# GEGLU feed-forward on one core: w_gate's first quarter in two transfers, x's second half released one transfer earlier in ACT's program

## The chip, the cores and the metric

The kernel runs on one core of a Trainium2 chip. The metric is the device time in microseconds (us) of one execution; the number quoted for a kernel is the median of several runs. Engines are named as the profile names them: PE (TensorE, matmuls; PEld is its weight loads), DVE (VectorE), ACT (ScalarE), POOL (GpSimd), SP (SyncE). A trailing q (ACTq, SPq) means the engine's instruction queue, which also issues DMA transfers.

## The reference

```python
B, S, D, F = 32, 32, 1024, 3584          # all bfloat16
def reference(x, w_gate, w_up, w_down):
    return (gelu_tanh(x @ w_gate) * (x @ w_up)) @ w_down
```

x is flattened to 1024 rows of D = 1024. w_gate and w_up are 1024 x 3584, w_down is 3584 x 1024.

## The kernel before, in words

The three products are done by a fast (Strassen-like, seven-product) scheme on two-by-two blocks. For the first two matrices the blocks are: x's first 512 rows and its other 512 rows, by the first and second half of D. In the code xt0 holds the transposed first 512 rows: B11 is its first half of D (KH = 4 steps of 128, called dt), B21 its second half. xt1 holds the other 512 rows (B12, B22). The 28 blocks of 128 columns of F (FT = 28) are the outer loop. A tile of w_gate, WG[c], holds 256 columns, so two blocks, with 8 dt; its first four dt meet B11 and its last four meet B21. A third stage multiplies by w_down.

The schedule is written out by hand: each engine executes its instructions in the order of the program text, and the queues of SP and ACT issue their transfers in that order as well. Semaphores are put in for data that one engine waits for from another.

The start, which is where the change lies, goes as follows.

- **SP** issues the transposing load of x's first half, B11 (L131). Its next transfer is the transposing load of x's second half, B21 (L149); after that come w_gate 2's second half, half of w_up 0, w_gate 3's second half, w_gate 4, the transposing load of xt1 (L154), w_gate 5 in two halves and the rest of w_up 0.
- **PE** runs NWARM = 10 matmuls on constants (L137), numbered n = 0 to 9, into four PSUM tiles in turn.
- **ACT** copies a little of warm product 1 into `table` (L139), which also holds its queue until that product is done. Then it issues six loads of w_gate (line L86 in the helper `load_gate`): w_gate 0's dt 0 and 1 (128 KB), its dt 2 and 3 (128 KB), the first four dt of w_gate 1, 2 and 3 (256 KB each), and w_gate 0's last four dt (256 KB). Then a second copy (L139 again, n = 8) waits for warm product 8, a copy of eight columns from `table` into B21 (L147) follows, and a Gelu on constants (L148) makes ACT load its Gelu table.
- The copy into B21 is called the *touch* below. The touch writes into the tile that x's second half is loaded into, so SP has to wait for it before it issues L149. It is what sets the moment of that load.
- **PE** then does `first_products(0, 1, cuts=(0, 2, KH))` (L279): blocks 0 and 1, both on w_gate 0, side by side: dt 0 and 1 of block 0, dt 0 and 1 of block 1, then dt 2 and 3 of each. All these matmuls have the line L195, in the helper `pair_product`. ACT copies each finished product to E1 (L212) and issues w_gate 1's second half (L280). Blocks 2 to 7 follow one by one with four matmuls each, so the first products of blocks 0 to 7 are 32 matmuls. Then `second_products(0)` to `second_products(7)` add B21 times the second half of each w_gate tile; the results go through Gelu on ACT (L219).
- **DVE** meanwhile makes sums of w_gate and w_up for blocks 0 and 1 (L175 to L184) and, once xt1 has landed, the sums T1 to T4 of the blocks of x (L166), which the remaining products read.

Of the kernel before, what the change touches and what calls it, by code (L numbers as in the profile page):

```python
# [7 lines left out]
ACT = mybir.ActivationFunctionType  # L8
# [4 lines left out]
def kernel(  # L13
# [18 lines left out]
    nc = tc.nc  # L32
# [11 lines left out]
    KH = DT // 2  # L44
# [31 lines left out]
    B11, B21 = xt0[:, :KH, :], xt0[:, KH:, :]  # L76
# [6 lines left out]
    def load_gate(c, queue, lo=0, hi=DT):  # L83
        if c not in WG:
            WG[c] = gw.tile([P, DT, 2 * P], bf16, name="gw", tag="gw")
        queue.dma_start(  # L86
            out=WG[c][:, lo:hi, :], in_=wg_r[:, lo:hi, 2 * c * P : (2 * c + 2) * P]
        )
# [12 lines left out]
    def a11(i):  # L101
        return block(WG, 2, i, 0)
# [21 lines left out]
    def psum_p(name):  # L124
        return psum.tile([P, NB], fp32, name=name, tag="p")

    def psum_q(name):
        return psum.tile([P, NB], fp32, name=name, tag="q")

    with tc.manual_schedule():  # L130
        nc.sync.dma_start_transpose(out=B11, in_=xf[0:NB, 0 : KH * P])  # L131
        ones = nc.const_aps.tensor(1.0, [P, NB], bf16)
        warm = [psum_p("warm") for _ in range(4)]
        table = opool.tile([P, 8], bf16, name="table", tag="o")

        for n in range(NWARM):
            nc.tensor.matmul(warm[n % 4], lhsT=ones[:, 0:P], rhs=ones, start=True, stop=True)  # L137
            if n in (1, 8):
                nc.scalar.activation(table, warm[n % 4][:, 0:8], ACT.Copy)  # L139
            if n == 1:  # L140
                load_gate(0, nc.scalar, 0, 2)
                load_gate(0, nc.scalar, 2, KH)
                for c in (1, 2, 3):
                    load_gate(c, nc.scalar, 0, KH)
                load_gate(0, nc.scalar, KH, DT)
            if n == 8:
                nc.scalar.activation(B21[:, 0, 0:8], table, ACT.Copy)  # L147
                nc.scalar.activation(table, ones[:, 0:8], ACT.Gelu_apprx_tanh)  # L148
        nc.sync.dma_start_transpose(out=B21, in_=xf[0:NB, KH * P : D])  # L149
        load_gate(2, nc.sync, KH, DT)  # L150
# [12 lines left out]
        def t_sum(name, a, b, step=2):  # L163
            for k in range(0, KH, step):
                ks = slice(k, k + step)
                nc.vector.tensor_tensor(T[name][:, ks, :], a[:, ks, :], b[:, ks, :], ALU.subtract)  # L166
# [24 lines left out]
        def pair_product(ps, lhs, rhs, first, cuts):  # L191
            for lo, hi in zip(cuts, cuts[1:]):
                for p, l in zip(ps, lhs):
                    for k in range(lo, hi):
                        nc.tensor.matmul(  # L195
                            p,
                            lhsT=l[:, k, :],
                            rhs=rhs[:, k, :],
                            start=(first and k == 0),
                            stop=(k == KH - 1),  # L200
                            skip_group_check=True,
                        )

        def first_products(*blocks, cuts=(0, KH)):
            for i in blocks:
                A[i] = psum_p("a") if 4 <= i < 8 else psum_q("a")
            pair_product([A[i] for i in blocks], [a11(i) for i in blocks], B11, True, cuts)
            for i in blocks:
                if i % 2 == 0:
                    pool, tag = (xpool, "e1") if i == LEAD - 2 else (ring, "ring")  # L210
                    E1[i // 2] = pool.tile([P, 2, NB], fp32, name="e1", tag=tag)
                nc.scalar.activation(E1[i // 2][:, i % 2, :], A[i], ACT.Copy)  # L212
# [63 lines left out]
        t_sum("T2", B22, T["T1"])  # L276
        t_sum("T3", B22, B12)
        t_sum("T4", B21, T["T2"])
        first_products(0, 1, cuts=(0, 2, KH))  # L279
        load_gate(1, nc.scalar, KH, DT)  # L280
        for n in range(2, 8):
            first_products(n)
# [39 lines left out]
        for i in range(2, FT + 1):  # L322
# [24 lines left out]
            if here and i % 2 == 0:  # L347
                c = i // 2 + (6 if i < 8 else 4)
# [8 lines left out]
        for i in range(RING):  # L357
            lo, hi = 4 * i, min(4 * i + 4, KF)
            nc.sync.dma_start(out=V11[i][:, : hi - lo, :], in_=wd_r[:, lo:hi, 0:DB])
        for j in range(JF):  # L360
            lo = KF + 2 * j
# [31 lines left out]
        B21 = lambda j: V21[j]  # L393
# [149 lines left out]
```

## Time and profile before

| | |
|---|---|
| median of 3 runs | 275.68 us (275.56 to 275.73) |
| the profiled execution | 275.76 us, of which the span of its instructions is 273.9 us |
| granted TensorE clock (mean) | 1.000 |
| PE busy | 268.7 us |
| ACT busy | 139.7 us |
| DMA read and written | 22.02 MB, 2.10 MB |
| warm matmuls start | 0.77 us |
| first real matmul starts | 5.41 us |
| second products start | 12.99 us |

All later times are from the start of the span. A line of the timeline has start, duration, engine, source line, operation, what is written and read, and in brackets how long the engine stood idle before it and what ended that idleness. In the chain of waits a line has start, duration and what held the end of the program in that time. A transfer has a time of issue, which is when its instruction starts on its queue, and a time of landing, which is when its semaphore is raised; the trace records both, and the starts of the single packets between them. The end of a matmul is modelled: matmuls overlap, and in a steady stream of these shapes they start 0.216 us apart though each is drawn 0.38 us long. An idle time of PE in a view is counted from the modelled end and is therefore shorter than the time lost between starts.

### The profile page before, as it was taken

The page shows a single profiled execution, that of the slowest core. Times are in us where ns is not written, and L with a number is a line of the kernel's source. Part 1 is how long each engine was busy: PE and PEld are TensorE (multiplying, and loading weights), DVE is VectorE, ACT ScalarE, POOL GpSimd, SP SyncE. Part 2 cuts the span into 40 slices and gives each one's busy share as a digit, 9 for nine tenths or more (in the row PEclk, how much of TensorE's full clock was granted, in tenths as well). Part 3 has the DMA queues.
Part 4 walks back from the last instruction along what each step waited for, and adds up shares of the span by engine and source line. Part 5 has one row for each costly group of instructions (what it writes and reads, how often), then busy time and mean ns, then how long its engine had stood idle before and what let it go on. Part 6 is the DMA issues. An engine that isn't in the chain of part 4 may idle for free.

```text
span 273.9 us, 3338 instructions
## 1 busy us (share of the span) xinstructions
PE 268.7 (98%) x1172; PEld 189.4 (69%) x1186; DVE 189.2 (69%) x226; ACT 139.7 (51%) x240; POOL 87.2 (32%) x81
## 2 busy tenths in 40 slices
PE   8999999999999999999999999999999999999995
PEld 2445677778777787776877768764447888888883
DVE  0078885866658666586665866769994999999900
ACT  4778665566565665666655666531100072860311
POOL 0000075745557455584555845600000000000000
PEclk9999999999999999999999999999999999999999
DMA  7999402153300034216360202369602000000321
GB/s 185 277 288 247 154 1 77 52 180 110 121 2 0 0 103 130 77 35 196 96 213 0 77 5 74 107 190 334 214 0 77 2 0 1 0 2 0 116 77 38
DMA packets 41024, 26.42 MB, mean 96 GB/s; under 512 B 9264, under 2 KB 41008, under 8 KB 41008
## 3 DMA queue, kind: packets, MB, share of 16 engines
q1 hardware_dynamic: 37680, 24.51, 30.5%
q10 hardware_dynamic: 3328, 1.70, 2.3%
q8 instruction: 9, 0.15, 0.2%
q14 instruction: 7, 0.06, 0.1%
HBM read 22.02 MB, written 2.10 MB: 88 GB/s over the span
## 4 chain that ended last, share of the span: by engine, by line
PE 94%; DMA 4%; ACT 1%; issue 0%
PE x L195 19%; PE x L398 18%; PE y L115 18%; PE a L195 15%; PE y L398 9%; PE x L115 9%; PE z L398 4%; DMA xt<-in_x_dram 3%; DMA gw<-in_w_gate_dram 1%; PE y L195 1%; ACT L139 0%; ACT o_sb L510 0%
## 5 line engine op out<-in xcount | busy, mean ns | idle before, releaser
L195 PE MATMUL x<-T,s 128*128 128x512 f32 x224 | 63.4, 407 | 0.0
L195 PEld LDWEIGHTS x<-T,s 128*128 128x128 f32 x224 | 41.7, 188 | 10.9 <-ACT e L242 0.3
L195 PE MATMUL a<-xt,gw 128*128 128x512 bf16 x182 | 44.1, 380 | 1.1 <-DMA xt<-in_x_dram 0.3
L259 DVE TENSOR_TENSOR u<-y,e 128x512 bf16<-128x512 f32 x28 | 19.3, 691 | 31.8 <-ACT e L257 30.9
L184 POOL TENSOR_TENSOR s<-gw,s 128x512 fp32r<-128x512 bf16 x22 | 26.0, 1182 | 47.6 <-PE y L115 46.9
L180 DVE TENSOR_TENSOR s<-s,gw 128x512 fp32r<-128x512 f32 x24 | 34.9, 1456 | 0.0
L195 PEld LDWEIGHTS <-gw 128*128 128x128 bf16 x192 | 17.1, 98 | 24.8 <-issue 5.2
L266 ACT ACTIVATE gl<-h 128x512 bf16<-128x512 bf16 x28 | 17.7, 631 | 27.5 <-DVE h L264 27.5
L246 DVE TENSOR_TENSOR gT<-gl,x 128x512 bf16<-128x512 bf16 x28 | 19.2, 686 | 17.9 <-PE x L115 17.9
L115 PE MATMUL x<-T,c 128*128 128x512 f32 x112 | 30.3, 392 | 0.0
L115 PE MATMUL y<-B,s 128*128 128x512 f32 x112 | 30.2, 391 | 0.0
L175 POOL TENSOR_TENSOR s<-uw 128x512 fp32r<-128x512 bf16 x25 | 29.1, 1165 | 0.0
L115 PE MATMUL y<-T,s 128*128 128x512 f32 x104 | 27.8, 389 | 0.0
L398 PE MATMUL x<-tc,sc 128*128 128x512 f32 x112 | 25.7, 389 | 0.0
L257 ACT ACTIVATE e<-x 128x512 f32<-128x512 f32 x28 | 16.7, 600 | 16.0 <-PE x L195 16.0
L176 POOL TENSOR_TENSOR s<-gw,uw 128x512 fp32r<-128x512 bf16 x21 | 24.5, 1167 | 0.0
L115 PEld LDWEIGHTS y<-B,s 128*128 128x128 f32 x112 | 21.0, 188 | 4.8
L212 ACT ACTIVATE e<-a 128x512 f32<-128x512 f32 x28 | 16.6, 597 | 15.2 <-PE a L195 15.2
L115 PEld LDWEIGHTS x<-T,c 128*128 128x128 f32 x112 | 20.9, 188 | 4.8 <-ACT e L257 0.4
L398 PEld LDWEIGHTS x<-tc,sc 128*128 128x128 f32 x112 | 21.0, 188 | 4.4
L115 PEld LDWEIGHTS y<-T,s 128*128 128x128 f32 x104 | 19.5, 188 | 4.1
L219 ACT ACTIVATE gl<-a 128x512 bf16<-128x512 f32 x28 | 16.7, 597 | 7.1 <-PE a L195 7.0
(58 smaller groups left out, 342.0 us busy)
## 6 DMA issues: line engine op xcount, KB each, us to landing
uw<-in_w_up_dram SPq DMA_DIRECT2D x6, 1024.0 KB, 6.4
gw<-in_w_gate_dram SPq DMA_DIRECT2D x8, 512.0 KB, 4.0
v<-in_w_down_dram SPq DMA_DIRECT2D x5, 512.0 KB, 3.8
v<-in_w_down_dram SPq DMA_DIRECT2D x4, 640.0 KB, 8.1
v<-in_w_down_dram SPq DMA_DIRECT2D x8, 256.0 KB, 4.2
out_dram<-o_sb SPq DMA_DIRECT2D x15, 128.0 KB, 1.7
gw<-in_w_gate_dram ACTq DMA_DIRECT2D x5, 256.0 KB, 5.0
uw<-in_w_up_dram SPq DMA_DIRECT2D x2, 512.0 KB, 5.4
```

Of the source, the lines that this page charges most:

```text
L115: nc.tensor.matmul(ps, lhsT=lhs[:, k, :], rhs=rhs[:, k, :], start=(first and k == 0), stop=(k == KH - 1), skip_group_check=True,)
L175: engine.tensor_tensor(S1[i], a21(i), a22(i), ALU.add)
L176: engine.tensor_tensor(S3[i], a11(i), a21(i), ALU.subtract)
L180: nc.vector.tensor_tensor(S2[i], S1[i], a11(i), ALU.subtract)
L184: engine.tensor_tensor(S4[i], a12(i), S2[i], ALU.subtract)
L195: nc.tensor.matmul(p, lhsT=l[:, k, :], rhs=rhs[:, k, :], start=(first and k == 0), stop=(k == KH - 1), skip_group_check=True,)
L219: nc.scalar.activation(GL[i // 2][:, i % 2, :], A[i], ACT.Gelu_apprx_tanh)
L246: nc.vector.tensor_tensor(gT[:, i, 0:NB], GL[i // 2][:, i % 2, :], X[i], ALU.mult)
L257: nc.scalar.activation(e3, X[i], ACT.Copy)
L259: nc.vector.tensor_tensor(U1[i], Y[i], e3, ALU.add)
L266: nc.scalar.activation(G1[i], h1, ACT.Gelu_apprx_tanh)
L398: nc.tensor.matmul(ps, lhsT=lhs[:, i, t * P : (t + 1) * P], rhs=rhs[:, i, :], start=(first and j == 0 and i == 0), stop=(last and j == JF ...
```

## The change

Three edits, all in the first microseconds of the program.

1. w_gate 0's first four dt are loaded in three transfers, not two: dt 0 alone (64 KB), dt 1 alone (64 KB), dt 2 and 3 (128 KB).
2. `first_products(0, 1)` is cut at each of the first two dt: dt 0 of block 0, dt 0 of block 1, dt 1 of block 0, dt 1 of block 1, then dt 2 and 3 of each. Number and kind of matmuls are the same.
3. The second copy from a warm product (n = 8) is dropped, and the touch of B21 is moved in ACT's program from behind all the w_gate loads to behind w_gate 2's first half. Behind it come w_gate 3's first half, w_gate 0's second half and the Gelu on constants.

```diff
         for n in range(NWARM):
             nc.tensor.matmul(warm[n % 4], lhsT=ones[:, 0:P], rhs=ones, start=True, stop=True)
-            if n in (1, 8):
-                nc.scalar.activation(table, warm[n % 4][:, 0:8], ACT.Copy)
             if n == 1:
-                load_gate(0, nc.scalar, 0, 2)
-                load_gate(0, nc.scalar, 2, KH)
-                for c in (1, 2, 3):
-                    load_gate(c, nc.scalar, 0, KH)
+                nc.scalar.activation(table, warm[n][:, 0:8], ACT.Copy)
+                for lo, hi in ((0, 1), (1, 2), (2, KH)):
+                    load_gate(0, nc.scalar, lo, hi)
+                load_gate(1, nc.scalar, 0, KH)
+                load_gate(2, nc.scalar, 0, KH)
+                nc.scalar.activation(B21[:, 0, 0:8], table, ACT.Copy)
+                load_gate(3, nc.scalar, 0, KH)
                 load_gate(0, nc.scalar, KH, DT)
-            if n == 8:
-                nc.scalar.activation(B21[:, 0, 0:8], table, ACT.Copy)
                 nc.scalar.activation(table, ones[:, 0:8], ACT.Gelu_apprx_tanh)
...
-        first_products(0, 1, cuts=(0, 2, KH))
+        first_products(0, 1, cuts=(0, 1, 2, KH))
```

## The prediction

> **What bounds the kernel now.** I read the page's head first. TensorE (PE) is busy for 98% of the span, so a change pays only through the few moments at which PE stands still. PE's waits come next, in the second fence.
>
> ```profile
> span 273.9 us, 3338 instructions
> PE 268.7 (98%) x1172; PEld 189.4 (69%) x1186; DVE 189.2 (69%) x226; ACT 139.7 (51%) x240; POOL 87.2 (32%) x81
> ```
> ```profile
> PE a L195 <- DMA xt<-in_x_dram: 0.3, 1, 0.3
> PE a L195 <- DMA gw<-in_w_gate_dram: 0.2, 1, 0.2
> ```
>
> These two lines are all that PE waits for from 5 to 13.1 us (total, times, longest); from 13 us to the end the same view has only the tail of the x wait. So all that can be won lies ahead of 13 us. The chain of waits, 0 to 20 us, says by what:
>
> ```profile
> 1.83 3.54 DMA gw<-in_w_gate_dram
> 5.37 0.05 issue
> 5.41 0.26 PE a L195
> 5.67 7.18 DMA xt<-in_x_dram
> 12.86 0.14 issue
> 12.99 1.67 PE a L195 x7
> ```
>
> w_gate's first piece lands at 5.37 and the products begin; x's second half, issued at 5.67, lands at 12.86, and the second products begin at 12.99. The timeline shows who does what in between:
>
> ```profile
> 2.29 2.83 ACTq L86 DMA_DIRECT2D gw<-in_w_gate_dram  x5
> ...
> 5.23 0.18 ACT L139 ACTIVATE table<-warm 128x8 bf16<-128x8 f32 x1 [3.03 <-PE warm L137]
> 5.41 7.30 PE L195 MATMUL a<-xt,gw 128*128 128x512 bf16 x32 [0.21 <-DMA gw<-in_w_gate_dram]
> 5.44 0.21 ACT L147 ACTIVATE xt<-table 128x8 bf16<-128x8 bf16 x1
> 5.67 3.97 SPq L149 DMA_TRANSPOSE xt<-in_x_dram  x1
> ```
>
> The touch of B21 (L147) runs 5.44 to 5.65, and SP issues x's second half at 5.67. The 32 first products start 0.216 us apart; the last starts at 12.33, so PE could start the second products at 12.55. They start at 12.99: **0.44 us lost to x**. Within the first products PE loses 0.17 us before w_gate 0's dt 2 and 3 (landed 6.41) and 0.03 before w_gate 1 (landed 7.31).
>
> Last, the DMA queues by stretch (q10 is ACT's, q1 is SP's): first the answer for 4.4 to 8.5 us, then for 9.3 to 11.0.
>
> ```profile
> q10 hardware_dynamic: 2400, 1.19, 111.4%
> ```
> ```profile
> q1 hardware_dynamic: 1540, 0.39, 107.9%
> ```
>
> Between 4.4 and 8.5 not one packet of x moves, though x was issued at 5.67 and the first half of x had its first packet 1.41 us after its issue. Between 9.3 and 11.0 only x moves, though w_gate 1's second half was issued on ACT at 7.54. The transfers go one after the other, in the order of issue, across both queues. In the trace the w_gate pieces land at 5.37, 6.41, 7.31, 8.21, 9.12 and, for w_gate 0's second half, 9.88; then x.
>
> **The change, part by part.**
>
> *The split quarter.* The first piece has half the bytes. Its packets cannot start before 4.21, when x's first half leaves the engines. Before, 128 of w_gate's packets (64 KB) were through by 4.49 and 256 by 4.70, and the landing came 0.6 after the last; so the new first piece lands near 5.1 (x's first half: 4.97) and the second at 5.4. Two matmuls run in each step, then PE waits for dt 2 and 3 as before. This early start is worth nothing: from w_gate 1's landing at 7.31 there are 24 matmuls, 7.36 + 24 x 0.216 = 12.54, which is already the end of the first products. Only an earlier w_gate 1 would move it. The extra transfer delays what is queued behind it by an amount that I call delta. Upper bound: the 128 KB piece landed 1.04 after the piece before it, where 256 KB pieces come 0.90 apart; by bytes it should be 0.45, so a boundary between small pieces may cost 0.59. Lower bound: that pause belongs to the start of the stream and not to the boundary, and smaller pieces fill it; w_gate 1 would then land up to 0.45 sooner. The later boundaries show none of it, and 64 KB of w_gate's packets took 0.27 us: I take delta = 0.1, nearer to the rows of the long stream.
>
> *The issues on ACT.* One more issue goes ahead of w_gate 1. Five took 2.83 us, 0.57 each. Packets of a plain load follow their issue by 1.05 us in a quiet stretch (40.8); w_gate 1's would be issued near 3.5 and is not due on the engines until about 5.2. Covered by 0.6 us.
>
> *The touch.* It no longer waits for the ninth warm matmul (3.03 us of idle ACT), and follows five issues in place of six and that wait: 1.83 + 0.43 + 4 x 0.57 = 4.54, and 0.24 for the touch: x can be issued at 4.8 (4.5 if the 64 KB issues are as short as 0.37, the shortest in the trace, 5.0 if as long as 0.64). One thing limits this. The trace gives each transfer a semaphore for its landing; the first eight have eight different ones and the ninth has the first's again. With one transfer more, x's second half or w_gate 0's second half is the ninth, and would wait until x's first half lands, 4.97. So x is issued at 4.8 to 5.1. The copy that is dropped (0.18) ran on an idle ACT: nothing.
>
> *The order of the transfers.* w_gate 3's first half is issued from 4.56 on, beside the touch, so still ahead of x; w_gate 0's second half follows at about 5.13, now behind x. x moves ahead of one transfer worth 0.76 to 0.91 us, and lands at about 12.0 instead of 12.86. PE asks for it at 12.55 + delta: 0.5 us of cover. The whole 0.44 goes.
>
> *What is late next.* w_gate 0's second half is needed at 12.55 too. It follows x, whose packets end at 11.03 - 0.85 = 10.2; 0.82 for its packets and 0.73 to its landing (what w_gate 1's second half took at 11.01): 11.7, cover 0.8. w_gate 1's second half keeps its place (12.58; needed at 12.55 + 8 x 0.216 = 14.3). SP is freed sooner, since x's issue holds it until the queue ahead drains (9.65 before), but all it issues then queues on engines that are busy anyway. The Gelu table load (5.67) stays behind two issues, 4.56 + 2 x 0.57 = 5.7; its cover is that the first result comes at 7.08.
>
> *Does it reach the end?* After 13 us PE waits for nothing. The nearest deadline is VectorE's chain on x's other rows, landed 21.43: the fourth T1 quarter is done at 24.02 and PE reads it near 25.4; the first half of T2 at 25.16 for 26.74. PE can come 1.3 us earlier before anything there decides.
>
> Sum against the profiled execution (275.76 us, span 273.9, 1.9 around it): -0.44 + 0.1 = -0.34. Against the median of 275.68: **275.35**, -0.12%. A measurement of this kernel can tell about 0.2%, 0.55 us, from no change.
>
> **The rivals.**
>
> *The stream starts better (faster).* If the pause at the first boundary goes, w_gate 1 lands at 6.9 to 7.1 and the first products end at 12.1 to 12.35; x at 12.0 just keeps up. -0.44 - 0.2 to -0.45: 274.8 to 275.05. For it: DMA throughput falls from 370 to under 200 GB/s in the 0.4 us after the first piece, and a stretch so thin need not recur. Against: w_gate's bytes ahead of w_gate 1 stay the same.
>
> *x passes w_gate 3 as well (slower).* w_gate 3 is issued only some 0.2 us before x. If x is taken first, its packets (2.4 us, 8.6 to 11.03) go between w_gate 2 and 3. It decides once w_gate 3 lands after 10.8, when PE reaches its 25th product. x from 7.5 to 9.9, 0.82 for w_gate 3, 0.73 to the landing: 11.5. Second products start at 11.5 + 0.05 + 8 x 0.216 = 13.3: +0.3. With x as late as 7.9 and the landing lag that x itself had (1.0, after 0.75 between its last data and its semaphores) 12.3 and +1.1. Middle +0.6: 276.25. Against it: the order of issue held throughout the trace.
>
> *Each small piece pays its boundary (no change, or slower).* With delta at its upper bound of 0.59, w_gate 1 lands at 7.9, the first products end at 13.13 and x is there long before: 13.13 against 12.99, +0.15: 275.85. For it stands the 1.04 us of the one 128 KB piece, against it the full rate at all later boundaries.
> The Trainium skill leans this way: its page "DMA: Bandwidth & Descriptors", section "Bandwidth", calls transfers under 64 KB dominated by descriptors and has 64 KB take 0.95 us (loads issued from GpSimd there). By that, an estimate, two pieces would hold w_gate 1 up by some 0.9 us and make it 276.15; the 0.27 us above disagrees.
>
> *x stays last (no change).* w_gate 0's second half is issued at about 5.1, x between 4.8 and 5.1; a plain load has packets after 1.05 us and x after 1.41. If readiness and not issue sets the order, x gains nothing but the gap of 0.35 us in its own stream near 9.5: 275.4 to 275.8.
>
> **How the numbers follow.** Forecast 0.38, better stream 0.26, x ahead of w_gate 3 0.17, small pieces 0.09, x last 0.10. Faster by over 0.2% (below 275.13): nearly all of the better stream and a small part of the forecast with a negative delta, 0.30. Slower by over 0.2% (above 276.23): over half of x ahead of w_gate 3 (0.10), and 0.08 for a delta at or above its upper bound together with a w_gate 3 or x that is late as well, 0.18. Within: 0.52. Range 274.8 to 276.25: the better stream's end, and the middle of the slower case, which leaves out about 0.1 above and less below; the forecast's own range is 275.15 to 275.7.
>
> **What would show it.** Right: x's second half issued at 4.8 to 5.1 with the wait for warm gone from ACT, x landing near 12.0, PE's x wait gone, second products starting at 12.6. First matmul near 5.15 and a longer wait for w_gate inside the first products show that the split gives nothing. Wrong: w_gate 1 landing more than 0.2 us away from 7.31, a PE wait near 10.8 for w_gate 3, x packets still behind w_gate 0's second half, or a new PE wait after 13 us.

## The result and the profile after

The changed kernel takes 280.00 us (median of six, 278.50 to 281.13) against 275.71 us: 1.0145 times as long, 95% interval 1.0105 to 1.0184. The forecast of 275.35 and its range were wrong. The profiled execution, 278.50 us, is the fastest of the six; the rest of this section reads it, and the clock, further down, makes the others longer.

The head of the page and PE's waits over the whole span (total, times, longest), as shown of before:

```profile
span 276.7 us, 3338 instructions
PE 267.8 (97%) x1172; PEld 189.3 (68%) x1186; DVE 189.3 (68%) x226; ACT 139.4 (50%) x239; POOL 87.2 (32%) x81
```
```profile
PE a L194 <- DMA xt<-in_x_dram: 2.8, 1, 2.8
PE a L194 <- DMA gw<-in_w_gate_dram: 1.2, 2, 0.8
```

PE's wait for x, 0.3 us before, was to vanish; it is 2.8 us. In the chain of waits (start, duration, holder) the transposing load of x's second half took 7.18 us from issue to landing before; now:

```profile
4.50 0.21 ACT xt L144
4.70 0.03 ACTq L86
4.73 10.86 DMA xt<-in_x_dram
15.59 0.14 issue
15.73 1.67 PE a L194 x7
```

x is issued 0.94 us sooner and lands 2.73 us later. The second products start at 15.73 instead of 12.99, +2.74, and the span is longer by just that (276.68 - 273.94): after that point nothing changes. The timeline has the neighbours:

```profile
4.51 1.05 ACTq L86 DMA_DIRECT2D gw<-in_w_gate_dram  x2
4.73 4.17 SPq L148 DMA_TRANSPOSE xt<-in_x_dram  x1
...
5.27 1.90 PE L194 MATMUL a<-xt,gw 128*128 128x512 bf16 x8 [0.85 <-DMA gw<-in_w_gate_dram]
```

The two issues on ACT are w_gate 3's first half, 4.51, and w_gate 0's second half, 5.05: 0.31 us behind x. The DMA queues from 9.3 to 11.0 us, where before only x moved (q1, 1540 packets):

```profile
q1 hardware_dynamic: 637, 0.16, 80.8%
q10 hardware_dynamic: 290, 0.15, 49.1%
```

x (q1) and ACT's w_gate loads (q10) move side by side, and both slowly: 0.31 MB in this stretch against 0.39 before. In the trace's packet records, x's 256-byte packets take 18 ns each in an undisturbed stretch and up to 80 here, w_gate's 27 and up to 116. w_gate 0's second half lands at 14.40 (9.88 before) and w_gate 1's at 15.31 (12.58).

The kernel before had such a stretch too, a short one, between the two that the prediction shows. From 8.5 to 9.3 us its queues moved:

```profile
q1 hardware_dynamic: 474, 0.12, 131.9%
q10 hardware_dynamic: 174, 0.08, 42.4%
```

Two things together make x late. Its data take longer: the last packet of x ends at 13.31 (11.10 before). And its landing waits another 2.28 us after that: x lands 0.28 us after w_gate 1's second half, as it also did before (12.58 and 12.86). The section on the landing lag shows that this is no coincidence.

### The profile page after: what moved, and what is told of

Same layout as the page of the kernel before. It is cut to its first block, busy times and chain, and to the rows that moved or that the text cites. A ratio compares the mean times of both kernels' runs of the same rounds, so it can differ in the third digit from the quotient of the medians.

```text
span 276.7 us, 3338 instructions
## 1 busy us (share of the span) xinstructions
PE 267.8 (97%) x1172; PEld 189.3 (68%) x1186; DVE 189.3 (68%) x226; ACT 139.4 (50%) x239; POOL 87.2 (32%) x81
## 4 chain that ended last, share of the span: by engine, by line
PE 93%; DMA 4%; ACTq 1%; ACT 1%; issue 0%
PE x L194 19%; PE x L397 18%; PE y L115 18%; PE a L194 15%; PE y L397 9%; PE x L115 9%; PE z L397 4%; DMA xt<-in_x_dram 4%; ACTq L86 1%; PE y L194 1%; ACT L139 0%; ACT o_sb L509 0%; ACT xt L144 0%
## 5 line engine op out<-in xcount | busy, mean ns | idle before, releaser
L194 PEld LDWEIGHTS x<-T,s 128*128 128x128 f32 x224 | 41.7, 188 | 10.9 <-ACT e L241 0.3
```

Of the source, the lines that this page charges most:

```text
L194: nc.tensor.matmul(p, lhsT=l[:, k, :], rhs=rhs[:, k, :], start=(first and k == 0), stop=(k == KH - 1), skip_group_check=True,)
```

## The experiments

In the tables "x" is x's second half and "behind" is how long behind x's issue ACT issues a plain load of w_gate. All times in us are from each kernel's profiled execution; before has x issued at 5.67, one load 1.87 behind, x landed at 12.86. Ratios are to the kernel before, run on the same chip beside it (its medians: 275.36 to 275.50).

### Which part, and is it the load behind x?

**e1_split_only**: the kernel before with edits 1 and 2 alone.

```diff
-                load_gate(0, nc.scalar, 0, 2)
-                load_gate(0, nc.scalar, 2, KH)
+                for lo, hi in ((0, 1), (1, 2), (2, KH)):
+                    load_gate(0, nc.scalar, lo, hi)
...
-        first_products(0, 1, cuts=(0, 2, KH))
+        first_products(0, 1, cuts=(0, 1, 2, KH))
```

> Part one alone: w_gate 0's first four dt in three transfers and the finer cuts; the touch of B21 stays behind all loads and the second warm copy, as before. Mixing theory (a plain load that ACT issues just behind x's transposing load shares the DMA engines with it and both crawl): no such load here, so x's second half keeps its place behind all of ACT's loads, lands at 12.9 to 13.1, and the time is 275.5 to 276.0. Rival, the split (the third small transfer or the semaphore it takes holds the stream up): x lands near 15.5 and the time is 278.5 or more. Rival, early issue (x suffers from being issued while several loads stand in the queue): as the mixing theory, 275.5 to 276.0.

**e2_move_only**: the changed kernel without edits 1 and 2.

```diff
-                for lo, hi in ((0, 1), (1, 2), (2, KH)):
+                for lo, hi in ((0, 2), (2, KH)):
...
-        first_products(0, 1, cuts=(0, 1, 2, KH))
+        first_products(0, 1, cuts=(0, 2, KH))
```

> Part two alone: the touch behind w_gate 2's first half and no second warm copy, with w_gate 0's first four dt in two transfers as before. Mixing theory and early-issue rival: x's second half is issued near 4.3, w_gate 0's second half right behind it; x lands at 15 to 15.7, PE waits 2.5 to 3.2 us for it, time 278 to 281. Split rival: as before or better, 275.2 to 275.7.

**e3_w_gate_0_behind_x**: the changed kernel, w_gate 0's second half on SP.

```diff
-                load_gate(0, nc.scalar, KH, DT)
...
+        load_gate(0, nc.sync, KH, DT)
         load_gate(2, nc.sync, KH, DT)
```

> The changed kernel with one transfer moved: w_gate 0's second half is issued on SP, right behind x's second half on the same queue, instead of on ACT. x is issued as early as in the changed kernel (4.7). Mixing theory: nothing of ACT's is issued behind x until w_gate 1's second half at about 7.2, which did not mix before; x's packets run alone after w_gate 3's, x lands at 11.8 to 12.2, w_gate 0's second half at about 12.7, time 275.2 to 275.6. Early-issue rival: x is slow all the same and lands after 14.5, time 277.5 or more.

**e4_w_gate_1_right_behind_x**: the kernel before, w_gate 1's second half issued earlier.

```diff
                 nc.scalar.activation(B21[:, 0, 0:8], table, ACT.Copy)
+                load_gate(1, nc.scalar, KH, DT)
...
-        load_gate(1, nc.scalar, KH, DT)
```

> The kernel before with one transfer moved: w_gate 1's second half is issued on ACT right behind the touch (near 5.7, as x is issued) instead of at 7.54. x is issued at 5.67 as before and all else is as before. Mixing theory: its packets share the engines with x's; x lands at 15 or later instead of 12.86 and the time is 277.5 to 280. Early-issue rival and split rival: nothing changes for x, 12.86, time 275.5 to 275.9.

| | x issued | behind | x landed | ratio (95%) |
|---|---|---|---|---|
| e1 | 6.12 | 1.48 | 12.85 | 1.0046 (1.0023 to 1.0070) |
| e2 | 4.29 | 0.31, 3.16 | 14.54 | 1.0115 (1.0088 to 1.0142) |
| e3 | 4.74 | 2.96 | 12.45 | 1.0011 (1.0002 to 1.0021) |
| e4 | 5.87 | 0.23 ahead of x | 12.36 | 1.0023 (1.0006 to 1.0040) |

e1 took longer than its theory allows (276.81 us); x came 0.46 us earlier than expected in e2, and 0.25 us later in e3.

The move is the larger part (e2); the split leaves x where it was (e1) but is not free. With the load that followed x at 0.31 us moved to SP, and x issued just as early, most of the loss is gone (e3). In e3's queues from 9.0 to 10.5 us x has the engines to itself:

```profile
q1 hardware_dynamic: 1374, 0.35, 126.8%
q10 hardware_dynamic: 4, 0.00, 0.4%
```

e4 missed its aim: ACT's queue does not wait for the touch, so the load went out ahead of x and was served ahead of it. It says only that a load ahead does no harm to x's landing.

### Keep the load, change its place

**e5_touch_behind_all_loads**: the changed kernel with the touch one place later.

```diff
-                nc.scalar.activation(B21[:, 0, 0:8], table, ACT.Copy)
                 load_gate(3, nc.scalar, 0, KH)
                 load_gate(0, nc.scalar, KH, DT)
+                nc.scalar.activation(B21[:, 0, 0:8], table, ACT.Copy)
```

> The changed kernel with the touch one more place later in ACT's program, behind w_gate 0's second half, so that x's second half is issued behind all of ACT's first loads, near 5.9, and still without the wait for warm. Order theory (a load that ACT issues within some tenths of a us after x's transposing load shares the engines with it and both crawl; a load issued before it is served first): nothing is issued behind x until w_gate 1's second half near 7.5; x lands at 12.6 to 13.0, and the time is 275.3 to 275.9. Early-issue rival (x crawls because it is issued while loads stand in the queue): as many loads stand in it, x lands after 14 and the time is 277.5 or more. If the split by itself costs something, this kernel is slower than the next-but-two (the same with two pieces) by as much.

**e6_w_gate_1_0.3_us_behind_x**: the kernel before; a second touch holds the load back.

```diff
                 nc.scalar.activation(B21[:, 0, 0:8], table, ACT.Copy)
+                nc.scalar.activation(WG[1][:, KH, 0:8], table, ACT.Copy)
+                load_gate(1, nc.scalar, KH, DT)
...
-        load_gate(1, nc.scalar, KH, DT)
```

> The kernel before, with w_gate 1's second half issued on ACT some 0.3 us behind x's second half instead of 1.9 us behind it: a second touch, of w_gate 1's own tile, holds its issue back until the touch of B21 has released x. (The run in which it was issued right behind the touch put it 0.23 us ahead of x, so it did not test this.) Order theory: the two crawl together, x lands after 14 instead of 12.86, PE waits 1.2 us or more for it, time 277 to 280. Early-issue rival: x is issued at 5.67 as before, nothing changes: 275.3 to 275.9.

**e7_w_gate_0_2.6_us_behind_x**: the changed kernel, w_gate 0's second half behind the Gelu table.

```diff
-                load_gate(0, nc.scalar, KH, DT)
                 nc.scalar.activation(table, ones[:, 0:8], ACT.Gelu_apprx_tanh)
+                nc.scalar.activation(WG[0][:, KH, 0:8], table, ACT.Copy)
+                load_gate(0, nc.scalar, KH, DT)
```

> The changed kernel with w_gate 0's second half held back on ACT until behind the Gelu table load, by a touch of its own tile: issued near 7.4, 2.6 us behind x's second half instead of 0.3. x is issued near 4.7 as in the changed kernel. Order theory: as with w_gate 1's second half at 1.9 us before, no sharing; x lands at 12.0 to 12.6, w_gate 0's second half at 12.2 to 12.8, time 275.2 to 276.0. Early-issue rival: x lands after 14.5, time 277.5 or more.

**e8_two_pieces_touch_behind_all**: e5 without the split.

```diff
-                for lo, hi in ((0, 1), (1, 2), (2, KH)):
+                for lo, hi in ((0, 2), (2, KH)):
...
-        first_products(0, 1, cuts=(0, 1, 2, KH))
+        first_products(0, 1, cuts=(0, 2, KH))
```

> The kernel before without the second warm copy and its wait: two pieces, touch behind all six of ACT's loads, Gelu behind it. x's second half is issued near 5.4 instead of 5.67. Order theory: nothing shares with x; it lands at 12.5 to 12.9; time 275.0 to 275.6, at best 0.3 us faster than before. Early-issue rival: x lands after 13.5, time 276.3 or more.

**e10_touch_0.4_us_longer**: the changed kernel, one line.

```diff
-                nc.scalar.activation(B21[:, 0, 0:8], table, ACT.Copy)
+                nc.scalar.activation(B21[:, 0, :], ones, ACT.Copy)
```

> The changed kernel with one edit: the touch of B21 is 512 columns wide instead of 8, so it takes 0.6 us instead of 0.2 and x's second half is issued near 5.1 instead of 4.73, within 0.1 us of w_gate 0's second half (5.05), which nothing else moves. Readiness theory: w_gate 0's second half is ready first and is served first, x behind it alone; x is issued 0.4 us later and lands 2.6 us or more sooner, at 12.3 to 13.0; w_gate 0's second half at 9.7 to 10.2; time 275.4 to 276.1. Rival, early issue: x still lands after 14.5, time 277.5 or more.

| | x issued | behind | x landed | ratio (95%) |
|---|---|---|---|---|
| e5 | 5.86 | 1.46 | 12.99 | 1.0036 (1.0016 to 1.0056) |
| e6 | 5.98 | 0.10 | 12.42 | 1.0006 (0.9990 to 1.0022) |
| e7 | 4.74 | 2.08, 2.75 | 13.10 | 1.0039 (1.0021 to 1.0056) |
| e8 | 5.40 | 1.97 | 12.46 | 1.0002 (0.9993 to 1.0010) |
| e10 | 5.15 | 0.10 ahead, 2.25 | 13.19 | 1.0044 (1.0030 to 1.0059) |

e10 is the plainest: the chain of waits of a kernel that issues x 0.42 us later than the changed one.

```profile
5.15 8.04 DMA xt<-in_x_dram
13.19 0.14 issue
13.32 1.67 PE a L194 x7
```

x lands 2.40 us sooner for being issued later, because w_gate 0's second half then goes first. e7 shows the other way out: the load stays on ACT and behind x, but at 2.08 us; x's data were through at 10.38. "Early issue" alone is therefore not the cause. Even so x landed only at 13.10, 0.28 us after w_gate 1's second half. e6 failed its expectation: at 0.10 us behind, the load still passed x (10.67 against 12.42). So order of issue is not what decides. It fits that a plain load needs less time from issue to first packet (1.05 us against 1.41 of a transposing load, in the trace of before), as the last rival of the prediction had it.

e5, e7 and e10 took 0.1 to 0.6 us longer than expected, in the median. e10's profiled execution, 276.00, is the fastest of its five (median 276.66). Among the eleven or twelve executions of e5 and e7 there is one each of 278.7 and 278.6 us with a clock of 0.994, as the changed kernel has it; no such execution of theirs was profiled. So these places make a long wait rare, but perhaps not impossible.

### How far behind, and how many

The kernel before with w_gate 1's second half at other distances: **e9**, **e11** and **e17** differ in what ACT does between the touch of B21 and the load.

```diff
                 nc.scalar.activation(B21[:, 0, 0:8], table, ACT.Copy)
+                nc.scalar.activation(table, table, ACT.Copy)             # e9: once, e11: four times
+                nc.scalar.activation(WG[1][:, KH, 0:8], table, ACT.Copy) # e17: WG[1][:, KH, :] from ones, alone
+                load_gate(1, nc.scalar, KH, DT)
...
-        load_gate(1, nc.scalar, KH, DT)
```

> The kernel before with w_gate 1's second half issued on ACT some 0.35 to 0.5 us behind x's second half (in the run at 0.10 us behind, it went ahead of x and x did not suffer). Readiness theory (a plain load has packets 1.05 us after its issue, a transposing load from 1.41 us on, over about as long as its own issue of 1.42 us takes; a plain load that becomes ready inside that stretch shares the engines with x and both crawl): it becomes ready in the first tenths of the stretch, as in the changed kernel; x lands at 14 or later, time 277 to 280. Rival, lateness by place (x suffers only when issued early, ahead of w_gate 0's second half): x lands by 13.0, time 275.3 to 275.9.

> The kernel before with w_gate 1's second half issued on ACT some 1.2 us behind x's second half. Readiness theory with a stretch of 1.4 us: it becomes ready 2.25 us after x's issue, inside the stretch from 1.41 to 2.8; the part of x that is ready later shares with it, x lands at 13.3 or later, time 276 to 279. If only a narrow stretch counts, x is served before it as with 1.9 and 2.1 us: x lands at 12.8 to 13.0, time 275.3 to 275.9.

> The kernel before with one load, w_gate 1's second half, issued on ACT some 0.3 us behind x's second half (a wider touch of its own tile than in the run that came out at 0.10 us); x is issued near 5.7 with all that was ahead of it still ahead. Delay theory: one load at 0.3 us is enough, as with w_gate 1 off ACT: x lands at 14 or later, time 276.7 to 279. Amount theory (one load costs little, two cost 1.2 us): x lands at 12.6 to 13.2, time 275.4 to 276.0.

**e15_two_loads_0.5_us_behind_x** is e9 with a second load.

```diff
+                load_gate(2, nc.scalar, KH, DT)
...
-        load_gate(2, nc.sync, KH, DT)
```

> The kernel before with two loads on ACT some 0.5 us behind x's second half: w_gate 1's second half as in the run at 0.48 us, and w_gate 2's second half right behind it, moved from SP. x is issued at 5.67 as before and has all it had ahead of it ahead of it. If the amount of sharing packets sets the loss: x lands at 13.5 or later, time 276 to 279. If the loss of the changed kernel needs x to be issued early, x lands by 13.0 and the time is 275.3 to 275.9.

In the changed kernel: **e14_w_gate_1_off_ACT** leaves w_gate 0's second half as the only load that can share, **e16_w_gate_0_0.75_us_behind_x** holds it back.

```diff
@@ e14
+        load_gate(1, nc.sync, KH, DT)
         load_gate(2, nc.sync, KH, DT)
...
-        load_gate(1, nc.scalar, KH, DT)
@@ e16
+                nc.scalar.activation(table, table, ACT.Copy)
+                nc.scalar.activation(WG[0][:, KH, 0:8], table, ACT.Copy)
                 load_gate(0, nc.scalar, KH, DT)
```

> The changed kernel with w_gate 1's second half moved from ACT to SP, behind x. So w_gate 0's second half still follows x by 0.3 us on ACT, but it is the only load that can share the engines with x. If x's lateness grows with the amount of plain packets that share with it (two loads of 512 packets in the changed kernel, one in the run at 0.48 us), x lands at 12.3 to 13.3 and the time is 275.6 to 276.6. Rival (one load that becomes ready in x's stretch is enough for the whole loss): x lands after 14.5, 277.5 or more.

> The changed kernel with w_gate 0's second half held back on ACT by a touch of its own tile, so that it is issued near 5.5, some 0.75 us behind x's second half instead of 0.31; x is issued at 4.73 as in the changed kernel, and w_gate 1's second half still follows on ACT. Delay theory (what counts is how soon behind x's issue the plain load comes: crawl at 0.3, little at 0.48, none from 1.2 on): x lands at 12.3 to 13.5, time 275.6 to 276.6. Rival (an early issue together with any load behind it): x lands after 14.5, 277.5 or more.

| | x issued | behind | x landed | ratio (95%) |
|---|---|---|---|---|
| e17 | 5.67 | 0.31 | 12.60 | 1.0026 (1.0008 to 1.0043) |
| e9 | 5.70 | 0.48 | 12.74 | 1.0019 (1.0003 to 1.0035) |
| e11 | 5.67 | 1.21 | 12.57 | 1.0005 (0.9995 to 1.0016) |
| e15 | 5.68 | 0.48, 0.97 | 14.02 | 1.0061 (1.0048 to 1.0074) |
| e14 | 4.73 | 0.32 | 15.41 | 1.0081 (1.0066 to 1.0095) |
| e16 | 4.74 | 0.80, 2.77 | 15.13 | 1.0143 (1.0112 to 1.0174) |

e15 has x at its old place and issue, and two loads close behind it are enough for a loss. Its chain of waits:

```profile
5.68 8.34 DMA xt<-in_x_dram
14.02 0.14 issue
14.15 1.67 PE a L198 x7
```

It is not x's data that the second load delays: they end at 12.19 in e15 and at 12.09 in e9. The second load, w_gate 2's second half, lands at 13.73, and x 0.29 us after it. With one load (e9, e17) packets share as well, and x's data end at about 12.0 instead of 11.1, but x then lands within 0.65 us; its landing is no later than before. The medians are still 0.1 to 0.3% above the kernel before, and the profiled execution of e17 (275.48) is the second fastest of nine (median 276.21), so others may have lost more.

In the changed kernel one load is enough (e14; its profiled execution, 278.95, is the slowest of four, median 277.83), at a distance of 0.80 us too (e16). So neither my amount theory nor my delay theory holds for both kernels, and the readiness theory of e9 and e11 missed as well. What the runs support: with x issued near 5.7, x and the load beside it lose little; from 9 to 13 us all queues together move 246 to 268 GB/s (e9, e15, e17; 265 before). With x issued at 4.29 to 4.74 and a load 0.3 to 0.8 us behind it, the same stretch has 150 to 219 GB/s (e2, e14, e16 and the changed kernel). That load then lands at 13.2 to 15.1, and x after it. In the profiled execution of e14 the start of x was jammed besides: single packets took up to 1.8 us between 7.5 and 9.0, and w_gate 3's first half landed at 10.69. Why the early issue makes one load so costly stays open. Sharing as such does not explain it: in e3 x is as slow from 9.0 to 9.5 us (141 GB/s, packets of up to 76 ns) with only three w_gate packets beside it.

### x's landing lag, the split, the clock

**e12_all_behind_x_on_SP** is e8 with w_gate 1's second half on SP.

```diff
+        load_gate(1, nc.sync, KH, DT)
         load_gate(2, nc.sync, KH, DT)
...
-        load_gate(1, nc.scalar, KH, DT)
```

> Two pieces, touch behind all six of ACT's loads without the second warm copy, and w_gate 1's second half issued on SP right behind x instead of on ACT. So no plain load of ACT's is near x at all. In the runs so far x's semaphores came only when the plain load issued on ACT behind it had gone through (before: x's last data at 11.03, its semaphores at 11.77). Theory: without it they come with the last data, near 10.8; x lands at 11.3 to 11.7, before PE has done the first products (12.35), PE does not wait for x at all; w_gate 1's second half lands near 12.2; time 274.9 to 275.3. Rival, the lag is x's own: x lands at 12.4, time 275.3 to 275.6.

x landed at 11.40 against 12.46 in e8, with its data through at nearly the same time: its landing no longer stands behind an ACT load. The traces show the same throughout (times in us):

| | end of x's data | last ACT load behind x lands | x lands |
|---|---|---|---|
| before | 11.10 | 12.58 | 12.86 |
| changed | 13.31 | 15.31 | 15.59 |
| e7 | 10.38 | 12.82 | 13.10 |
| e8 | 10.76 | 12.18 | 12.46 |
| e9 | 12.09 | 12.26 | 12.74 |
| e15 | 12.19 | 13.73 | 14.02 |
| e12 | 10.91 | none | 11.40 |

In 15 of the 20 profiled executions x lands 0.25 to 0.29 us after the last ACT load issued behind it. In the other five (e4, e6, e9, e12, e17) there is no such load, or it lands before or soon after the end of x's data, and x lands 0.47 to 0.65 us after its data. Moving that one load off ACT (e8 to e12) and adding one to ACT (e9 to e15) both move x's landing with it, so the landing waits for those loads. By this, an earlier x gains nothing in the changed kernel unless w_gate 1's second half lands earlier too.

PE did not wait for x in e12, as expected, but the time was not better, 1.0020 (1.0004 to 1.0035). Its PE waits show why:

```profile
PE a L195 <- DMA gT<-in_w_gate_dram: 0.8, 1, 0.8
```

SP is held by x's issue until 9.44, the load behind it starts late, the engines are partly idle from 10.9 to 11.5, and w_gate 5 comes too late at 23.6. No version tried beats the kernel before; e6, e8 and e11 cannot be told from it.

**e13_three_transfers_old_cuts** is e1 without the finer cuts.

```diff
-        first_products(0, 1, cuts=(0, 1, 2, KH))
+        first_products(0, 1, cuts=(0, 2, KH))
```

> The split's transfers alone: three transfers of w_gate 0's first four dt, but the products cut as before (first two dt in one step), touch and second warm copy as before. The kernel with the finer cuts as well was slower than before by 0.46%, with x's landing and the start of the second products where they were. If the third transfer is what costs, this one is slower by as much, 276.4 to 276.9; if PE's early start with pauses between is what costs, it is as before, 275.2 to 275.7.

Measured 1.0037 (1.0011 to 1.0063), near e1's ratio, but with a median of 275.85 us, which is between the two forecasts. Two of its twelve executions (278.92 and 279.30, clock 0.994) make half of the excess. So the finer cuts are not needed for a loss (e5 against e8 points the same way), but how much of it is the third transfer's is not shown; e3, which has the split, is at 1.0011. In the profiled executions the split moves the second products by 0.13 us in e13 (13.12) and by none in e1 (12.98). The rest is in executions whose cause these traces don't show. e1's profiled execution is one with another clock:

```profile
core 0: 276.5 us, clock 0.950
```

There bf16 matmuls follow each other at 0.224 us throughout, not 0.216, with the landings of before. The split is not needed for that: one execution of e4, which has no split, took 277.92 us at a clock of 0.948. What brings it about is open.

**e18_PE_kept_busy** is the changed kernel with block 7's first product done four times.

```diff
-            first_products(n)
+            first_products(n, times=4 if n == 7 else 1)
```

> The changed kernel with block 7's first product done four times over instead of once (12 more matmuls, 2.6 us, writing the same values), in the time in which PE waits for x; all transfers as in the changed kernel. The changed kernel's runs fall apart by the granted clock: 278.5 at 1.000, 279.6 to 281.1 at 0.993 to 0.994. Clock theory (PE's wait of 3 us lets the clock fall to half for some 3.4 us, which costs 1.1 to 2.6 us more than the wait): with PE busy the clock stays, and the median is 278.0 to 278.8. Rival (the spread is in the transfers): the median stays at 279.5 to 280.5.

Median 278.58 (278.42 to 279.75), 1.0119 (1.0099 to 1.0138). All five executions have a clock of 0.999 or 1.000, where five of the changed kernel's six have 0.993 or 0.994. So with PE busy the clock stays, as expected. The intervals of the two ratios overlap, and two of the five took 279.05 and 279.75 at the full clock, so the clock is not the whole of the spread. The fall itself is seen in e2's windows (PE, PEld, DVE, ACT and POOL busy, granted clock, DMA):

```profile
12.00:14.50 2.50, 0.59 (x3) 0.09 (x1) 0.00 (x0) 0.96 (x2) 0.00 (x0) 1.00 1.20 248
14.50:18.20 3.70, 3.52 (x9) 1.30 (x10) 1.17 (x2) 0.60 (x1) 0.00 (x0) 0.54 1.20 291
18.20:24.00 5.80, 5.80 (x29) 2.65 (x27) 4.62 (x9) 4.68 (x9) 0.00 (x0) 1.00 1.19 257
```

After PE's wait the clock is half for 3.41 us (14.63 to 18.04) and eight matmuls follow each other at 0.427 us: 8 x 0.211 = 1.7 us. e2's span is longer by 3.36: 1.69 for x and 1.67 for the clock. e16's profile has the same 3.41 us at half clock. The changed kernel's five longer runs have a mean clock of 0.993 or 0.994, which is 1.7 to 1.9 us of a span of 278. The Trainium skill, page "TensorE: Matmul & The Clock Gate", section "Part 1: The HAM clock gate (the "warmup" mystery)", has the clock fall to half after an idle window of about 3.4 us that runs freely. The 3.41 us here agree with the length of that window. That PE must be idle through all of it they do not bear out: in e2 the clock fell with matmuls starting only 2.47 us apart (12.21 and 14.68). It stayed at 1.000 with 3.20 us in the changed kernel's profiled execution and 3.30 us in e14. It may depend on where in the window the wait lies; no run here tests that.

## Why the prediction was wrong, point by point

- **The step that failed** is "The transfers go one after the other, in the order of issue, across both queues", and with it "x moves ahead of one transfer ... and lands at about 12.0". It has two errors. First, the loads that the change puts 0.31 and 2.48 us behind x moved beside it, and x's data ended at 13.31 (forecast 10.2). Second, the forecast let x land at 12.0, ahead of w_gate 1's second half at 12.58; but x's landing waits for ACT's loads behind it. e7 shows the second error by itself: x's data are through at 10.38, nearly as forecast, and x lands at 13.10. Together they made 15.59, 3.6 us off, which is the whole of the miss in the profiled execution. e3, e7 and e10 get most of it back by moving one load.
- **What the rows before had shown of it.** From 8.5 to 9.3 us both queues moved, and x landed 1.76 us after its data and 0.28 us after w_gate 1's second half. The prediction read the stretches on both sides and took x's lag to be x's own.
- The issue was nearly right: x at 4.73 (forecast 4.8 to 5.1). The wait of w_gate 0's second half for x's first half cost nothing: x's first half landed at 4.95, and ACT's queue issued w_gate 3 until 5.01 anyway. In e2, where that load has no such wait, it follows x by the same 0.31 us.
- **The split** gave nothing at the front, as said: first matmul at 5.27, but w_gate 1 at 7.50, delta = 0.19 against 0.1. One execution does not size delta: over all kernels profiled, w_gate 1 landed at 6.80 to 7.31 with two transfers and at 6.81 to 7.57 with three. That e1, e5 and e13 are 0.36 to 0.46% slower than before was in none of the terms.
- **"What is late next"** failed with the order: w_gate 0's second half at 14.40 (forecast 11.7), w_gate 1's at 15.31 (12.58). PE waited for neither, since x landed behind both.
- **The rivals.** "x passes w_gate 3" was partly there: w_gate 3 landed at 9.88 instead of 9.12, within its cover. "x stays last" had the right idea, that readiness and not issue sets the order (e6), but assumed that the two could not overlap. No rival had two queues sharing, though the Trainium skill states it: "DMA: Bandwidth & Descriptors", section "Queues, rings and completion order", has each engine take turns between queues by packets. The trace agrees in that both queues' packets move in the same stretch, from 9 to 13 us; how the turns go it does not show.
- **"After 13 us PE waits for nothing"** held: 2.74 us of later start are 2.74 us of span.
- **The clock** was missing. I priced a wait by its length; a wait near 3 us costs another 1.7 us in most executions, which makes 280.0 out of 278.5.

## What to carry to other kernels

Before a transposing load is released earlier, look at what another queue issues behind it. Here its landing came after the landing of those loads, wherever they landed later than its data, so data that arrive sooner are worth nothing by themselves. Plain loads up to 0.8 us behind an early x slowed the whole stream besides. Putting them ahead of x (e10), on its own queue (e3) or 2 us later (e7) got most of the loss back, but no version came out ahead of the kernel before. A trace shows the order of transfers only for the distances that occur in it, and only in the stretches that one reads. And price a TensorE wait of 2.5 to 3 us with the fall of the clock that can follow it.

## What the runs showed of the hardware that was not expected

- x's transposing load alone moved 289 GB/s with 18 ns a packet; beside plain loads of another queue the two together moved 178 GB/s (0.71 MB from 9 to 13 us of the changed kernel). With x issued near 5.7 the two lost little (e17: 268 GB/s in that stretch, 265 before).
- Two plain loads of different queues sharing did not slow each other: from 13.5 to 14.0 us of the changed kernel w_gate on both queues had packets of at most 44 ns, at 290 GB/s.
- A transposing load landed 0.25 to 0.29 us after the last plain load issued behind it on ACT's queue, in 15 of 20 profiled executions, up to 2.7 us after its own data (e7). Without such a load it landed 0.49 us after its data (e12).
- The granted clock can stand at 0.949 through a whole execution (e1): bf16 matmuls 0.224 us apart, float32 ones unchanged at 0.227.
